# A linear-attention recurrence in blocks: mask on VectorE, scores from 64 rows a head, bonus sums and a compact state on TensorE

## The chip, the core and the metric

The kernel runs on one core of a Trainium2 chip. The metric is the device time of one execution in microseconds (us). A core has TensorE (matrix products into PSUM, with a separate stream of weight loads), VectorE, ScalarE, GpSimd (which can't read PSUM), and SyncE, whose queue (SP) here issues most DMAs.

## The reference

Three stages follow each other: a recurrence with a decaying state (4 batches, 8 heads, 768 steps, head size 48), a mixture of experts with fixed capacity, and a second one with a router over argmax. Only the first matters here:

```python
state = np.zeros((B, H, D, D)); y = np.zeros_like(r)
for t in range(S):
    kt, vt, rt, wt = (k[:, :, t], v[:, :, t], r[:, :, t], w[:, :, t])
    cur = np.einsum('bhd,bhe->bhde', u[None] * kt, vt)
    y[:, :, t] = np.einsum('bhd,bhde->bhe', rt, state + cur)
    state = wt[:, :, :, None] * state + np.einsum('bhd,bhe->bhde', kt, vt)
```

The first expert stage then needs all 3072 rows of y and their gate logits, since its tokens are chosen by a search for a threshold over all rows.

## The kernel before

The recurrence is cut into 24 blocks (`NB`) of 128 steps (`C`), 6 for each batch. Within a block the decay is written as products: `suf` is the suffix product of w (a reversed scan on VectorE), `pf` the prefix product divided by the whole block's product (a second scan), `rp` = r x pf, `kh` = k x suf. Partitions hold 2 heads of 64 (48 used) channels, and 4 such pairs (`NP`) stand side by side, so channel tiles are 128 x 4 x 128. All products on TensorE are fp32.

For block j the steps are, by the functions in `attention`:

- `load`, `load2`: SP fetches channel data (`ch`: w, k, r in two half-height parts, then v for the logits) into one of 3 buffers and token data (`tk`: v, r, k by rows) into one of 4.
- `prep` (L95): the two scans, `rp`, `kh` (GpSimd), the block's product `pe`, and the largest |w| into `WM` for a range check at the end of the kernel.
- `prep2` (L120): ScalarE copies `rp` into a block-diagonal tile `rbd`, so that one 128-row product gives the scores of two heads apart.
- `scores` (L135): 4 products of 256 columns into `pa` (2 banks of PSUM, 2 buffers), 4 transposes of `kh`; ScalarE copies both out (`am`, `kt`). `mask` (L150): GpSimd zeroes `am` above the diagonal.
- `bonus`, `cbv`: r x u x k by rows on GpSimd (`ru`), its sum for each head on VectorE (`cb`), and cb x v on ScalarE, 8 small products (`cv`).
- `vw` (L154): gate logits of v, 3 products, written beside v. `kv` (L171): the state's update: 4 products into `pv`, added to the decayed state on VectorE in two half-height instructions, multiplied by the next block's `pe` on GpSimd (`tmp`, 448 columns, half of them zero).
- `out` (L193): 4 products with the state and 8 with the masked scores into `py` (one buffer), then logits (`le`, `L`) and rows (`y`) on VectorE, and an SP store into DRAM.

The loop over j runs `kv(j)`, `prep(j+2)`, `scores(j+1)`, `mask(j+1)`, `prep2(j+2)`, `vw(j+2)`, `bonus(j+2)`, `out(j)`, `cbv(j+1)`. Each engine works through its instructions in the order in which this code issues them; an instruction that waits holds up those behind it on the same engine. Between the last blocks stand the first steps of the search (`S.mark`, `S.count`, `S.narrow`), and behind the loop the expert stages, whose order is written out by hand with fixed paces.

## Time and profile before

| what | us |
|---|---|
| median of 3 timed runs | 816.48 (812.16 to 817.46) |
| the profiled execution | 810.52 |
| its span, first to last instruction | 808.8 |
| VectorE, busy in the span | 631.8 |
| TensorE, busy in the span | 713.9 |
| GpSimd, busy in the span | 413.1 |
| ScalarE, busy in the span | 352.1 |

The recurrence takes up the first part of the span, to about 233 us, the expert stages the rest. Busy time of an engine includes what an instruction waits after it has started. A share over the whole span says little, since the two parts have different limits; the recurrence is read by itself. Fp32 products appear as two records each, transposes as one.

### The profile page before, as it was taken

The numbers are of one execution on the slowest core, as the hardware profiler recorded it, in microseconds if no ns is written. First come the engines' busy times: TensorE is split into PE (matmuls) and PEld (weight loads), VectorE is DVE, ScalarE is ACT, GpSimd is POOL, SyncE is SP. The second block draws the span as 40 slices with busy tenths as digits, with TensorE's granted clock in tenths as the row PEclk, the third lists the DMA queues.
The fourth block names the chain that finished last, engine by engine and source line by source line (L and its number), as shares of the span: only waits on it lengthen the run. The fifth ranks groups of instructions, "written<-read, shape, count | busy, mean of one in ns | idle before, by whom it ended". The sixth has DMA issues, their size and how long they took to land.

```text
span 808.8 us, 13793 instructions
## 1 busy us (share of the span) xinstructions
PE 713.9 (88%) x4889; PEld 633.7 (78%) x4889; DVE 631.8 (78%) x1575; ACT 352.1 (44%) x756; POOL 413.1 (51%) x371
## 2 busy tenths in 40 slices
PE   6887778878787798999999999999999999999993
PEld 4776667777754577878787878878778999999993
DVE  7999999999978877687876866847776668677770
ACT  3454545545422224333332433323345556666650
POOL 5788876878715413121211212135558766776640
PEclk8898988889899999999999999999999999999998
DMA  8567767667305235251533424264438766776740
GB/s 284 137 177 174 192 163 183 172 173 193 89 31 186 88 99 173 74 183 50 170 104 112 143 74 157 59 206 138 152 126 288 243 224 218 254 255 219 237 161 24
DMA packets 35199, 129.08 MB, mean 160 GB/s; under 512 B 5225, under 2 KB 14580, under 8 KB 35120
## 3 DMA queue, kind: packets, MB, share of 16 engines
q0 software_dynamic: 17568, 83.82, 30.8%
q1 hardware_dynamic: 16832, 43.95, 20.0%
q8 instruction: 40, 0.66, 0.4%
q10 hardware_dynamic: 720, 0.34, 0.2%
q14 instruction: 39, 0.32, 0.1%
HBM read 113.88 MB, written 14.60 MB: 159 GB/s over the span
## 4 chain that ended last, share of the span: by engine, by line
PE 48%; DVE 30%; issue 10%; DMA 5%; POOL 3%; ACT 2%; POOLq 0%; SPq 0%; DVEq 0%; ACTq 0%
PE ph L837 18%; PE po L710 9%; DVE pf L110 5%; PE po L712 4%; PE po L714 4%; PE po L713 4%; DVE suf L104 3%; DMA ch<-in_ch 2%; DVE pe L116 2%; DMA wraw<-in_w1b,wi 2%; DVE pc L107 2%; PE px L1190 2%; DVE rp L112 2%; DVE g L997 2%; PE px L1010 1%
## 5 line engine op out<-in xcount | busy, mean ns | idle before, releaser
L841 ACT ACTIVATE hh<-ph 128x256 fp32r<-128x256 f32 (+3 forms) x160 | 68.4, 428 | 223.4 <-PE ph L837 204.4
L837 PE MATMUL ph<-xh,w1h 128*128 128x256 f32 (+1 forms) x480 | 154.4, 322 | 1.0 <-DVE hl L845 1.0
L837 PE MATMUL ph<-xl,w1h 128*128 128x256 f32 (+1 forms) x480 | 146.2, 305 | 0.5 <-DVE xl L785 0.2
L837 PE MATMUL ph<-xh,w1l 128*128 128x256 f32 (+1 forms) x480 | 146.3, 305 | 0.0
L139 PE MATMUL pa<-rbd,kh 128*128 128x256 f32 x192 | 64.8, 496 | 46.2 <-ACT rbd L125 46.2
L837 PEld LDWEIGHTS ph<-xh,w1h 128*128 128x128 f32 x480 | 90.6, 189 | 10.6 <-issue 5.0
L837 PEld LDWEIGHTS ph<-xl,w1h 128*128 128x128 f32 x480 | 90.8, 189 | 3.1 <-DVE xl L785 1.4
L710 PE MATMUL po<-w2h,hh 128*128 128x384 f32 x272 | 93.1, 489 | 0.0
L837 PEld LDWEIGHTS ph<-xh,w1l 128*128 128x128 f32 x480 | 90.8, 189 | 0.0
L845 DVE SCALAR_TENSOR_TENSOR hl<-ph,hh 128x256 fp32r<-128x256 f32 (+1 forms) x108 | 49.7, 461 | 51.2 <-ACT hh L841 46.7
L139 PEld LDWEIGHTS pa<-rbd,kh 128*128 128x128 f32 x192 | 45.3, 248 | 56.5 <-POOL ru L131 43.0
L713 PE MATMUL po<-w2l,hh 128*128 128x384 f32 x264 | 88.5, 335 | 0.0
L753 ACT CAST w1h<-wraw 128x768 fp32r<-128x768 f32 x88 | 73.2, 833 | 12.5 <-DMA wraw<-in_w1a,ix 8.8
L498 POOL DMA_INDIRECT wraw<-in_w1a,ix x16 | 16.5, 1034 | 121.3 <-issue 53.0
L710 PEld LDWEIGHTS po<-w2h,hh 128*128 128x128 f32 x272 | 49.5, 190 | 28.8
L757 DVE TENSOR_TENSOR w1l<-wraw,w1h 128x768 fp32r<-128x768 f32 x66 | 64.6, 979 | 7.6 <-ACT w1h L753 7.4
L498 POOL DMA_INDIRECT xg<-xd,ix x24 | 31.3, 1305 | 76.2 <-DVE ix L1146 61.1
L757 POOL TENSOR_TENSOR w1l<-wraw,w1h 128x768 fp32r<-128x768 f32 x22 | 41.2, 1876 | 49.5 <-ACT w1h L753 49.4
L169 ACT ACTIVATE cv<-tk,cb 128x56 f32<-128x56 f32 x192 | 47.2, 328 | 39.2 <-DVE cb L166 39.2
L757 DVE TENSOR_TENSOR w2l<-wraw,w2h 128x768 fp32r<-128x768 f32 x44 | 47.8, 1086 | 11.5 <-ACT w2h L753 11.5
L712 PE MATMUL po<-w2h,hh 128*128 128x384 f32 x160 | 55.2, 345 | 0.0
L714 PE MATMUL po<-w2h,hl 128*128 128x384 f32 x160 | 53.8, 337 | 0.1
(350 smaller groups left out, 1766.9 us busy)
## 6 DMA issues: line engine op xcount, KB each, us to landing
tk<-in_tk SPq DMA_DIRECT2D x24, 608.0 KB, 6.6
ch<-in_ch SPq DMA_DIRECT2D x42, 288.9 KB, 5.4
xd<-y SPq DMA_DIRECT2D x24, 193.0 KB, 2.7
x2d<-x SPq DMA_DIRECT2D x8, 579.0 KB, 4.1
ch<-in_ch SPq DMA_DIRECT2D x23, 192.0 KB, 5.8
ch<-in_ch SPq DMA_DIRECT2D x1, 962.5 KB, 8.8
ch<-in_ch SPq DMA_DIRECT2D x1, 770.5 KB, 8.9
ch<-in_ch SPq DMA_DIRECT2D x2, 256.0 KB, 5.1
```

What stands on the lines that cost most here:

```text
L139: nc.tensor.matmul(pa[:, 2 * a:2 * a + 2], t["kh"][:, a], t["rb"][:, a], start=True, stop=True)
L169: nc.scalar.mul(cv[:, h], t["v"][:, DE * h:DE * h + DE], cb[:, h:h + 1])
L498: nc.gpsimd.indirect_dma_start(out=out, out_offset=None, in_=src, in_offset=bass.IndirectOffsetOnAxis(ap=idx, axis=0), bounds_check=bound, ...
L710: mm(o, hh[:, s], w[0][:, hs], start=a, stop=z)
L712: mm(o, hh[:, s], w[0][:, hs], start=a, stop=False)
L713: mm(o, hh[:, s], w[1][:, hs], start=False, stop=False)
L714: mm(o, hl[:, s], w[0][:, hs], start=False, stop=z)
L753: nc.scalar.copy(hi, r)
L757: self.turn[j][q].tensor_tensor(lo, r, hi.bitcast(FT), OP.subtract)
L837: nc.tensor.matmul(ph, a[:, f // 4, k, s], b[:, k], start=(n == 0), stop=(n == 3 * KB - 1))
L841: nc.scalar.activation(hh, ph, AF.Relu)
L845: nc.vector.scalar_tensor_tensor(hl, ph, 0.0, hh.bitcast(FT), op0=OP.max, op1=OP.subtract)
```

## The change

VectorE multiplies the scores in PSUM by a 0/1 mask tile (`msk`) into `am`; the ScalarE copy and the GpSimd selection are gone. Scores are 8 products of 64 rows (one head each) and 128 columns, straight from `kh` and `rp`; `rbd` is gone. The bonus sum is r x k in channel layout (`rk`, GpSimd) times u on TensorE, 4 products of 2 columns, into the logits' bank, copied out with them by ScalarE. The token data loses r and k (1216 to 456 columns). The state is kept for each head in its own half of the partitions: 8 products of 64 weight columns into `pv`, one addition (`s`), one GpSimd product of 224 columns (`tmp`), and two ScalarE copies into a block-diagonal tile `bd` for `out`. The range check is two ScalarE passes with sums (`within`) in place of a reduce on VectorE. `prep` and `prep2` are cut anew, `out` is split into `out`, `logits` and `rows`, and the loop's order changes. The diff, cut:

```diff
...
-            tk = ld.tile([128, TW], FT, name="tk", bufs=4)
...
+            tk = ld.tile([128, VW], FT, name="tk", bufs=4)
             nc.sync.dma_start(tk, d["tk"][j])
-            t["v"], t["rk"] = tk[:, 0:VW], tk[:, VW:].rearrange("p (a c) -> p a c", a=2)
...
-            suf = wk.tile([128, NP, C + 1], FT, name="suf")
+            t["suf"] = suf = wk.tile([128, NP, C + 1], FT, name="suf")
             sufl = suf.rearrange("p a b -> p (a b)")
             nc.vector.tensor_tensor_scan(sufl[:, ::-1], w[:, 1:n + 1][:, ::-1], K["d1r"][:, ::-1], 0.0, OP.mult, OP.add)
             df = d1f[j % 2]
-            pc = wk.tile([128, NP], FT, name="pc")
-            nc.vector.tensor_scalar(pc, suf[:, :, 0], 2.0 ** -100, None, op0=OP.max)
-            nc.vector.reciprocal(df[:, :, 0], pc)
+            nc.vector.tensor_scalar(PE_[:, j], suf[:, :, 0], 2.0 ** -100, None, op0=OP.max)
+            nc.vector.reciprocal(df[:, :, 0], PE_[:, j])
+            t["kh"] = wk.tile([128, NP, C], FT, name="kh", bufs=2)
+            nc.gpsimd.tensor_tensor(t["kh"], k, suf[:, :, 1:], OP.mult)
+
+        def prep2(j):
...
-            nc.vector.tensor_tensor_scan(pf.rearrange("p a b -> p (a b)"), w[:, 0:n], df.rearrange("p a b -> p (a b)"), 0.0, OP.mult, OP.add)
+            nc.vector.tensor_tensor_scan(pf.rearrange("p a b -> p (a b)"), w[:, 0:n], d1f[j % 2].rearrange("p a b -> p (a b)"), 0.0, OP.mult, OP.add)
             t["rp"] = wk.tile([128, NP, C], FT, name="rp", bufs=3)
             nc.vector.tensor_tensor(t["rp"], r, pf[:, :, 0:C], OP.mult)
-            t["kh"] = wk.tile([128, NP, C], FT, name="kh", bufs=2)
-            nc.gpsimd.tensor_tensor(t["kh"], k, suf[:, :, 1:], OP.mult)
-            t["pe"] = wk.tile([128, NP], FT, name="pe", bufs=4)
-            nc.vector.tensor_copy(t["pe"], suf[:, :, 0])
-            nc.vector.tensor_copy(PE_[:, j], suf[:, :, 0])
-            nc.vector.tensor_reduce(WM[:, j:j + 1], w, axis=AX.X, op=OP.max, apply_absolute_value=True)
...
-        def prep2(j):
...
+        def rkm(j):
...
-            rb = rbd[j % 3]
-            t["rb"] = rb
-            nc.scalar.copy(rb[0:64, :, 0], t["rp"][0:64])
-            nc.scalar.copy(rb[64:128, :, 1], t["rp"][64:128])
-
-        def bonus(j):
...
-            rk = t["rk"]
-            ru = wk.tile([128, DM], FT, name="ru")
-            nc.gpsimd.tensor_tensor(ru, rk[:, 0], u, OP.mult)
-            nc.gpsimd.tensor_tensor(ru, ru, rk[:, 1], OP.mult)
-            t["ru"] = ru
+            w, k, r = cuts(j)
+            t["rk"] = wk.tile([128, NP, C], FT, name="rk")
+            nc.gpsimd.tensor_tensor(t["rk"], r, k, OP.mult)
...
+        def within(j):
+
+            w = T[j]["ch"][:, 0:CHW]
+            jk = wk.tile([128, CHW], BF, name="jk", bufs=1)
+            nc.scalar.activation(jk, w, AF.Relu, bias=wmax, accum_out=WM[:, 0, j:j + 1])
+            nc.scalar.activation(jk, w, AF.Relu, scale=-1.0, accum_out=WM[:, 1, j:j + 1])
 
         def scores(j):
             t = T[j]
-            pa = ps.tile([128, 2 * NP, C], FT, name="pa", bufs=2)
+            t["pa"] = pa = ps.tile([128, 2, NP, C], FT, name="pa", bufs=2)
             for a in range(NP):
-                nc.tensor.matmul(pa[:, 2 * a:2 * a + 2], t["kh"][:, a], t["rb"][:, a], start=True, stop=True)
+                for h in range(2):
+                    q = slice(64 * h, 64 * h + 64)
+                    nc.tensor.matmul(pa[:, h, a], t["kh"][q, a], t["rp"][q, a], start=True, stop=True)
...
-            t["am"] = am = wk.tile([128, 2 * NP, C], FT, name="am")
-            nc.scalar.copy(am, pa)
-            if j % NCH < NCH - 1:
...
         def mask(j):
-            am = T[j]["am"]
-            nc.gpsimd.affine_select(am, am, pattern=[[0, 2 * NP], [1, C]], compare_op=OP.is_gt, fill=0.0, base=0, channel_multiplier=-1)
+            t = T[j]
+            t["am"] = am = wk.tile([128, 2, NP, C], FT, name="am")
+            nc.vector.tensor_tensor(am.rearrange("p h a c -> p (h a) c"), t["pa"].rearrange("p h a c -> p (h a) c"),
+                                    msk[:, None, :].to_broadcast([128, 2 * NP, C]), OP.mult)
...
         def vw(j):
...
-            pl = ps.tile([128, H, E], FT, name="pl")
+            pl = ps.tile([128, H, E + 1], FT, name="pl")
             for a in range(3):
-                nc.tensor.matmul(pl, vt[:, a], wg[:, a], start=(a == 0), stop=(a == 2))
-            nc.scalar.copy(t["v"].rearrange("p (h e) -> p h e", e=DE)[:, :, D:], pl)
+                nc.tensor.matmul(pl[:, :, 0:E], vt[:, a], wg[:, a], start=(a == 0), stop=(a == 2))
+            for a in range(NP):
+                nc.tensor.matmul(pl[:, 2 * a:2 * a + 2, E:E + 1], t["rk"][:, a], us[:, a], start=True, stop=True)
+            nc.scalar.copy(t["v"][:, :, D:], pl)
...
         def cbv(j):
             t = T[j]
-            cb = wk.tile([128, H], FT, name="cb")
-            nc.vector.tensor_reduce(cb, t["ru"].rearrange("p (h d) -> p h d", d=D), axis=AX.X, op=OP.add)
             t["cv"] = cv = wk.tile([128, H, DE], FT, name="cv")
             for h in range(H):
-                nc.scalar.mul(cv[:, h], t["v"][:, DE * h:DE * h + DE], cb[:, h:h + 1])
+                nc.scalar.mul(cv[:, h], t["v"][:, h, 0:DE], t["v"][:, h, DE:DG])
...
         def kv(j):
...
+            t = T[j]
+            if j % NCH == NCH - 1:
...
+            t["pv"] = pv = ps.tile([128, H, DE], FT, name="pv")[:, 0:NP]
+            for a in range(NP):
+                for h in range(2):
+                    q = slice(64 * h, 64 * h + 64)
+                    nc.tensor.matmul(pv[q, a], t["kt"][:, a, q], t["v"][:, 2 * a + h, 0:DE], start=True, stop=True)
+
+        def state(j):
...
+            s = wk.tile([128, NP, DE], FT, name="s")
+            if c == 0:
+                nc.vector.tensor_copy(s, t["pv"])
+            else:
+                nc.vector.tensor_tensor(s, t["pv"], t["tmp"], OP.add)
...
+            t1["tmp"] = tmp = wk.tile([128, NP, DE], FT, name="tmp")
+            nc.gpsimd.tensor_tensor(tmp, s, t1["suf"][:, :, 0:1].to_broadcast([128, NP, DE]), OP.mult)
+            t1["bd"] = bd = bds[(j + 1) % 2]
             for h in range(2):
                 q = slice(64 * h, 64 * h + 64)
-                if c == 0:
-                    nc.vector.tensor_copy(s[q, :, h], pv[q, :, h])
-                else:
-                    nc.vector.tensor_tensor(s[q, :, h], pv[q, :, h], t["tmp"][q, :, h], OP.add)
-            tmp = wk.tile([128, NP, 2 * DE], FT, name="tmp")
-            pe = T[j + 1]["pe"]
-            nc.gpsimd.tensor_tensor(tmp, s.rearrange("p a h e -> p a (h e)"), pe[:, :, None].to_broadcast([128, NP, 2 * DE]), OP.mult)
-            T[j + 1]["tmp"] = tmp.rearrange("p a (h e) -> p a h e", h=2)
+                nc.scalar.copy(bd[q, :, h], tmp[q])
 
...
-                    nc.tensor.matmul(py[:, 2 * a:2 * a + 2], t["rp"][:, a], t["tmp"][:, a], start=True, stop=False)
+                    nc.tensor.matmul(py[:, 2 * a:2 * a + 2], t["rp"][:, a], t["bd"][:, a], start=True, stop=False)
                 for h in range(2):
                     o = 2 * a + h
-                    nc.tensor.matmul(py[:, o], t["am"][:, o], t["v"][:, DE * o:DE * o + DE], start=(c == 0), stop=(h == 1 or c == 0))
+                    nc.tensor.matmul(py[:, o], t["am"][:, h, a], t["v"][:, o, 0:DE], start=(c == 0), stop=(h == 1 or c == 0))
...
+        def logits(j):
...
+            nc.vector.tensor_tensor(le, t["py"][:, :, D:], t["cv"][:, :, D:], OP.add)
             nc.vector.tensor_reduce(L[:, j], le.rearrange("p h e -> p e h"), axis=AX.X, op=OP.add)
-            if j == NB - 1:
...
+        def rows(j):
...
-            nc.vector.tensor_tensor(y[:, 0:DM].rearrange("p (h d) -> p h d", d=D), py[:, :, 0:D], t["cv"][:, :, 0:D], OP.add)
...
+        msk = wk.tile([128, C], FT, name="msk", bufs=1)
+        nc.vector.tensor_scalar(msk, K["i32"], 0.0, None, op0=OP.is_gt)
+        us = wk.tile([128, NP, 2], FT, name="us", bufs=1)
+        nc.scalar.dma_start(us, d["us"])
...
+        for t in bds:
...
         prep(0)
         prep2(0)
+        rkm(0)
         load(2)
...
         for j in range(NB):
             if j + 3 < NB:
                 load(j + 3)
                 load2(j + 3)
+            if j + 1 < NB:
+                scores(j + 1)
             kv(j)
             if j == NB - 3:
-                spare = ps.tile([128, 2 * NP, C], FT, name="pa", bufs=2).rearrange("p a b -> p (a b)")
+                spare = ps.tile([128, 2, NP, C], FT, name="pa", bufs=2).rearrange("p h a b -> p (h a b)")
                 s0, s1 = spare[:, 0:512], spare[:, 512:1024]
             if j == NB - 2:
                 g = S.mark(wk, 0, n1, 0)
             if j + 2 < NB:
+                within(j + 2)
                 prep(j + 2)
             if j + 1 < NB:
-                scores(j + 1)
                 mask(j + 1)
             if j == NB - 3:
                 S.span2(wk, s0)
             if j + 2 < NB:
                 prep2(j + 2)
-                vw(j + 2)
-                bonus(j + 2)
+                rkm(j + 2)
             if j == 0:
                 meta_ready()
             out(j)
             if j + 1 < NB:
                 cbv(j + 1)
+            if j + 2 < NB:
+                vw(j + 2)
+            state(j)
+            logits(j)
+            if j == NB - 1:
+                S.count(s1, g, 0, n1)
+                for i in range(S.hot):
+                    nc.tensor.matmul(s0, K["ones"], K["q1"][:, None, :].to_broadcast([128, 4, 128]), start=True, stop=True)
+                S.count(s1, S.mark(wk, n1, NB, 1), n1, NB)
+            rows(j)
...
```

## Rows read from the trace of the kernel before

PE is TensorE, PEld its weight loads, DVE VectorE, ACT ScalarE, POOL GpSimd, SPq SyncE's queue; L104 is line 104 of the kernel before. In the table of stretches the engines come in the order PE, PEld, DVE, ACT, POOL, behind the stretch and its length.

**Rows 1.** Busy us and instructions by engine, granted clock, DMA share, GB/s, by stretch

```profile
0.00:20.00 20.00, 13.25 (x52) 8.91 (x53) 14.82 (x26) 7.43 (x17) 11.75 (x18) 0.83 0.86 284
...
100.00:120.00 20.00, 13.34 (x88) 12.24 (x88) 19.50 (x32) 10.23 (x27) 16.14 (x14) 0.87 0.66 176
...
240.00:260.00 20.00, 13.59 (x114) 7.64 (x114) 17.07 (x56) 4.03 (x7) 10.51 (x9) 1.00 0.50 166
```

**Rows 2.** Chain of waits: start us, length us, engine, tile, line; four suffix scans

```profile
19.98 1.24 DVE suf L104
...
103.84 1.25 DVE suf L104
...
113.21 1.24 DVE suf L104
...
213.66 1.24 DVE suf L104
```

**Rows 3.** Timeline 103 to 111 us, VectorE and GpSimd: start us, length us

```profile
105.77 1.17 POOL L114 TENSOR_TENSOR kh<-ch,suf 128x512 f32<-128x512 f32 x1
...
106.08 1.95 DVE L110 TENSOR_TENSOR_SCAN pf<-ch,d1f 128x516 f32<-128x516 f32 x1
...
106.89 2.02 POOL L152 TENSOR_SCALAR_AFFINE_SELECT am<-am 128x1024 f32<-128x1024 f32 x1
...
108.06 1.39 DVE L112 TENSOR_TENSOR rp<-ch,pf 128x512 f32<-128x512 f32 x1
...
108.88 1.42 POOL L131 TENSOR_TENSOR ru<-tk,u 128x384 f32<-128x384 f32 x1
...
109.38 0.96 DVE L116 COPY pe<-suf 128x4 f32<-128x4 f32 x1
```

**Rows 4.** Timeline near the recurrence's start and end, instructions that nothing holds up

```profile
9.08 0.69 DVE L112 TENSOR_TENSOR rp<-ch,pf 128x512 f32<-128x512 f32 x1 [1.81 <-DMA ch<-in_ch]
9.69 0.16 DVE L116 COPY pe<-suf 128x4 f32<-128x4 f32 x1
...
224.28 0.93 POOL L190 TENSOR_TENSOR tmp<-st,pe 128x448 f32<-128x448 f32 x1 [2.95 <-DVE st L187]
```

**Rows 5.** Groups by line, 40 to 200 us: shapes, count, busy us, mean ns

```profile
L118 DVE TENSOR_REDUCE WM<-ch 128x1 f32<-128x517 f32 x17 | 11.5, 678 | 0.0
...
L212 DVE TENSOR_TENSOR y<-py,cv 128x384 f32<-128x384 f32 x17 | 9.3, 547 | 0.0
...
L187 DVE TENSOR_TENSOR st<-pv,tmp 64x224 f32<-64x224 f32 x22 | 8.4, 383 | 0.1
L205 DVE TENSOR_REDUCE L<-le 128x8 f32<-128x64 f32 x17 | 4.6, 268 | 0.6
L204 DVE TENSOR_TENSOR le<-py,cv 128x64 f32<-128x64 f32 x17 | 3.8, 223 | 0.6
```

**Rows 6.** Timeline of TensorE's products, 119 to 134 us, half clock in the first row

```profile
120.24 3.75 PE L139 MATMUL pa<-rbd,kh 128*128 128x256 f32 x8 [4.11 <-ACT rbd L125]
...
125.40 0.43 PE L199 MATMUL py<-tmp,rp 128*128 128x112 f32 x2
...
128.07 1.10 PE L180 MATMUL pv<-tk,kt 128*128 128x112 f32 x8
129.01 1.91 PE L139 MATMUL pa<-rbd,kh 128*128 128x256 f32 x8
130.75 0.60 PE L143 MATMUL pk<-ident,kh 128*128 128x128 f32 x4
131.19 0.78 PE L160 MATMUL pl<-wg,ch 128*128 128x64 f32 x6
131.81 1.94 PE L202 MATMUL py<-tk,am 128*128 128x56 f32 x16
```

**Rows 7.** DMA issues: the row store's issue; all half-height loads, KB, us to landing

```profile
112.08 0.34 SPq L214 DMA_DIRECT2D xd<-y  x1
...
ch<-in_ch SPq DMA_DIRECT2D x42, 288.9 KB, 5.4
```

More of the change, by code (lines that the diff above doesn't have):

```diff
@@ L39 @@
 DE = D + E
-VW = H * DE
-TW = VW + 2 * DM
+DG = DE + 1
+VW = H * DG
+WMAX = 1.0625
 HOT = 12
@@ L72, in attention @@
         d1f = [wk.tile([128, NP, C + 1], FT, name=f"d1f{i}", bufs=1) for i in range(2)]
-        rbd = [wk.tile([128, NP, 2, C], FT, name=f"rbd{i}", bufs=1) for i in range(3)]
-        stt = [wk.tile([128, NP, 2, DE], FT, name=f"st{i}", bufs=1) for i in range(2)]
+        bds = [wk.tile([128, NP, 2, DE], FT, name=f"bd{i}", bufs=1) for i in range(2)]
         def load(j, *cuts):
@@ L171, in kv @@
         def kv(j):
             t = T[j]
+            if j % NCH == NCH - 1:
+                return
+            t["pv"] = pv = ps.tile([128, H, DE], FT, name="pv")[:, 0:NP]
[4 more added lines that the diff above has]
+        def state(j):
+            t = T[j]
             c = j % NCH
-            if c == 0:
-                t["tmp"] = None
@@ L176, in kv @@
             if c == NCH - 1:
                 return
-            pv = ps.tile([128, NP, 2, DE], FT, name="pv")
-            for a in range(NP):
-                nc.tensor.matmul(pv[:, a], t["kt"][:, a], t["v"][:, 2 * DE * a:2 * DE * a + 2 * DE], start=True, stop=True)
-            s = stt[j % 2]
+            s = wk.tile([128, NP, DE], FT, name="s")
[3 more added lines that the diff above has]
+                nc.vector.tensor_tensor(s, t["pv"], t["tmp"], OP.add)
@@ L195, in out @@
             c = j % NCH
[L196 removed]
+            t["py"] = py = ps.tile([128, H, DE], FT, name="py" if j < NB - 1 else "pv")
             for a in range(NP):
                 if c:
[L199 removed]
+                    nc.tensor.matmul(py[:, 2 * a:2 * a + 2], t["rp"][:, a], t["bd"][:, a], start=True, stop=False)
                 for h in range(2):
                     o = 2 * a + h
[L202 removed]
+                    nc.tensor.matmul(py[:, o], t["am"][:, h, a], t["v"][:, o, 0:DE], start=(c == 0), stop=(h == 1 or c == 0))
+        def logits(j):
+            t = T[j]
             le = wk.tile([128, H, E], FT, name="le")
[L204 removed]
+            nc.vector.tensor_tensor(le, t["py"][:, :, D:], t["cv"][:, :, D:], OP.add)
             nc.vector.tensor_reduce(L[:, j], le.rearrange("p h e -> p e h"), axis=AX.X, op=OP.add)
[L206 to L210 removed]
+        def rows(j):
+            t = T[j]
             y = wk.tile([128, XW], FT, name="y", bufs=3)
[L212 removed]
+            nc.vector.tensor_tensor(y[:, 0:DM].rearrange("p (h d) -> p h d", d=D), t["py"][:, :, 0:D], t["cv"][:, :, 0:D], OP.add)
             nc.gpsimd.tensor_copy(y[:, DM:XW], meta[:, j])
@@ L235, in attention @@
         meta, meta_ready = meta_load()
-        nc.gpsimd.memset(rbd[1], 0.0)
-        for t in stt:
+        for t in bds:
             nc.gpsimd.memset(t, 0.0)
@@ L246, in attention @@
         prep(1)
-        nc.gpsimd.memset(rbd[2], 0.0)
-        bonus(0)
         mask(0)
         prep2(1)
+        rkm(1)
         cbv(0)
         vw(1)
-        bonus(1)
+        within(0)
+        within(1)
         n0, n1 = NB - 3, NB - 2
@@ L313, in host @@
     uc[:, :, :D, 0] = u.reshape(NP, 2, D)
-    return dict(uc=uc.reshape(NP, 128, 1), ch=ch.reshape(NB, 128, CW), tk=tk, u=np.ascontiguousarray(u.reshape(1, DM)),
+    us = np.zeros((2, 64, NP, 2), np.float32)
+    for h in range(2):
+        us[h, :D, :, h] = u.reshape(NP, 2, D)[:, h].T
+    return dict(uc=uc.reshape(NP, 128, 1), us=us.reshape(128, NP, 2), ch=ch.reshape(NB, 128, CW), tk=tk.reshape(NB, C, VW),
                 wg=np.ascontiguousarray(wg.reshape(3, 128, H, E).transpose(1, 0, 2, 3)))
```

45 lines of the change are left out of this document (20 added, 25 removed).

## The prediction

> **What bounds the kernel now.** I read the table of stretches first. In the stretch from 100 to 120 us, which stands for the whole recurrence, VectorE is busy 19.50 of 20 us, TensorE 13.34, GpSimd 16.14 and ScalarE 10.23; the granted TensorE clock averages 0.87 [rows 1]. So the recurrence goes by VectorE. Next the chain of waits, for the period: one suffix scan (line 104) is followed by the next one after 113.21 - 103.84 = 9.37 us. From the scan of block 2 (19.98) to that of block 23 (213.66) there are 21 periods, 193.68 / 21 = 9.22 us on the mean [rows 2]. (The mean is lower because one block in six ends a sequence and has no state update.)
>
> Then the timeline, for what fills those 9.2 us. The reader should lay VectorE's rows beside GpSimd's. The prefix scan `pf` starts at 106.08 and shows 1.95 us; the GpSimd product `kh` runs from 105.77 to 106.94, and the scan ends 1.09 us after that. `rp` shows 1.39 us and ends at 109.45, 0.54 us after the GpSimd selection `am` (106.89 + 2.02 = 108.91). The four-column copy `pe` shows 0.96 us and ends with the GpSimd product `ru` (108.88 + 1.42 = 110.30) [rows 3]. At the start of the kernel, where GpSimd isn't in the way, the same `rp` takes 0.69 and the same `pe` 0.16 us [rows 4]. So a VectorE instruction with two SBUF inputs, or a small copy in SBUF, waits for the GpSimd instruction in progress: some 2.4 us of VectorE's "busy" time per block is such waiting (0.86 on `pf`, 0.70 on `rp`, 0.80 on `pe`). An instruction that reads PSUM doesn't show it: `le` has a mean of 0.223 us over 17 blocks [rows 5].
>
> **The change, part by part.** All figures are for one block; there are 22 periods that can shorten (block 2 to the end of iteration 21).
>
> *VectorE, what goes.* `pe` (0.96), the copy into `PE_` (0.16, by the uncovered `pe`), the range reduce `WM` (0.678), the bonus reduce `cb` (384 columns; by the range reduce's 517 in 0.678, 0.5), one of the two half-height state additions (0.383) [rows 3 to 5]: 2.7 us. *What comes*: the mask product of 1024 columns out of PSUM. No such row exists; `y` (384 columns, PSUM plus SBUF) takes 0.547 and `le` (64) 0.223, or 1.01 ns a column, so 1024 columns make 0.547 + 640 x 0.00101 = 1.20 us. Bounds: the columns alone, 1.04, and 1.40 if two PSUM banks cost a second fixed part of some 0.16; I take 1.20.
>
> *VectorE, what is left.* suf 1.25, two four-column instructions at 0.16, mask 1.20, pf 1.09, rp 0.54 to 0.69, state 0.383, le 0.223, L 0.268, y 0.547: 5.9 us in durations. What GpSimd still does is `kh` (1.17), the new r x k product of the same shape (1.17), and `tmp` with half its columns: 0.93 uncovered at 448 columns [rows 4], so 0.47 to 0.93, I take 0.5; selection and both `ru` are gone. `kh` can only start behind `suf`, then runs beside the mask, which reads PSUM. The r x k product follows it and ends some 2.4 us after `suf`; VectorE reaches `pf` some 1.6 us after `suf` (two small instructions and the mask), so about 0.8 us of waiting stays. 5.9 + 0.8 = 6.7 us. Bounds: 5.9 if nothing waits, and 8.1 if a small instruction waits for all of `kh` (1.0 more) and `suf` for `tmp` (0.4).
>
> *TensorE.* At the full clock, from start to start of the groups: output 128.07 - 125.40 = 2.67, state product 0.94, scores 1.74, transposes 0.44, logits 131.81 - 131.19 = 0.62; sum 6.41 us [rows 6]. Each fp32 product is two records, a transpose one, and an interval is about 0.11 us where the moving side has 128 columns or fewer. After: 16 score records of 128 columns, 1.78 us if they go one by one, 0.9 if the two 64-row halves go side by side. State product: 16 records with 64 weight columns, 1.76 if each costs what a 128-column one does, 0.47 if each costs half and two go at once. Four new products for the bonus sums are 8 records, 0.88. Transposes and output as before. Sum: 5.9 to 8.1. Where the form of the product changes (some four times a block) the overlap of one group with the next may be lost; the state product shows 1.10 us against 0.94 to the next start, so 0 to 0.16 each, 0.64 in all. One block in six has no transposes and state product, and one no state part in the output (2.67 against 1.94 - 0.16), which takes 0.3 to 0.5 off the mean. TensorE's mean then lies between 5.6 and 8.3 us; no row decides, and I take the middle, 7.0.
>
> The Trainium skill, on its page "TensorEngine Tiling (Array Packing)", sections Overview and Key Properties, says that products with at most 64 rows can run up to twice as fast as independent tiles, and also that changing the tiling mode drains the engine. By the first alone the sum would be near 6 us, by the second with nothing gained above 8; no run here shows either yet.
>
> *Clock.* Scores at half clock take 3.75 us instead of 1.91 [rows 6], and those come after waits of some 3 us for `rbd`. These waits go: 7.0 us of work in a period of about that length leaves none. From 240 to 260 us TensorE has only 13.59 busy us of 20 and the granted clock is 1.00 [rows 1], so short gaps don't lower it. I take the full clock.
>
> *ScalarE.* 10.23 of 20 us is 4.8 a block. It loses the copy of the scores (1024 columns) and two `rbd` copies (512 each), and gets two range passes (517 each) and two state copies (224 each): fewer columns, one instruction more. I cost it at nothing; its cover is the 2 us that it idles in a 7 us period. The Trainium skill, "ScalarE: Activation LUTs", section What ACT_TABLE_LOAD costs, gives 280 ns + 0.833 ns a column for an activation with a bias operand, 0.71 us for the first range pass; the sum would be the same, under the cover.
>
> *DMA and queues.* The token load shrinks from 128 x 1216 to 128 x 456 fp32, 608 to 228 KB; the count of DMAs per block stays five, all on SP. SP's load of block j+3 stands behind the row store of block j-1, as before, and takes 5.4 us to land; with three issues of 0.34 us (the store, the load's first two parts) that is 6.4 us, under 7 [rows 7]. At the start the two token loads ahead of block 2's load bring 0.76 MB less, at the 284 GB/s of the first 20 us [rows 1] 2.6 us: the scan at 19.98 should come at about 17.4. The new wait of that load for the range pass on ScalarE lies ahead of a need one period later.
>
> *New waits.* The mask makes VectorE wait for TensorE's scores (before, ScalarE did); behind it stand pf, rp, state, le, L and y. Scores of the next block need only last iteration's rp, and follow the logits, so they are early unless TensorE is the bound. TensorE's bonus products wait for r x k, which is done some 3 us ahead of them. The tail (block 23: marks, mask, output, count) keeps its length: the mask of 1.2 replaces a selection, but the state goes through one more engine.
>
> **Sum.** VectorE 6.7, TensorE 7.0 (5.6 to 8.3), loads 6.4. Two engines so near each other wait for one another at every block; I take 7.1 us a period. 22 x (9.22 - 7.1) = 46.6, plus 2.6 at the start: 810.5 - 49 = 761 for the profiled execution, which shows 810.52 with a span of 808.8. The three timed runs have a median 6 us above that execution and a lowest one 1.6 above; I put 4 on top: **765 us**.
>
> **Rivals.**
> 1. *TensorE becomes the bound, or the waits for GpSimd come back elsewhere.* 64-row records cost full ones and each change of form its 0.16, or a small VectorE instruction waits for `kh`: 8.1 to 8.3 us. For it: no row shows that half-height products cost less. Against: two independent upper ends. 22 x (9.22 - 8.2) = 22; 810.5 - 25 + 4 = 790 us. Chance 0.22.
> 2. *Everything pairs.* TensorE needs 5.6 to 6, `pf` gets ahead of r x k, and the period falls to the 6.4 us of the loads: 810.5 - 62.0 - 2.6 + 4 = 750 us. For it: r x k needs nothing of the scan and could be put anywhere; against: it is queued behind `kh`. Chance 0.12.
> 3. *The other side: the clock.* If the tiled products with few rows don't hold the clock at 2.4 GHz, TensorE's 7.0 us become 14 at 1.2 GHz throughout: 810.5 + 22 x 4.8 = 916 us. It decides from a mean granted clock of 7.0 / 9.22 = 0.76; the stage now has 0.87, with long waits in it that go away. Chance 0.04.
> 4. *The change gives back what it takes* (mask stalls on scores, state copy late, range passes in ScalarE's way), and the period stays over 8.9 us: 808 or more. Nothing on the page asks for it. Chance 0.03.
>
> **How the numbers follow.** 0.59 is left for the forecast, whose own range is 6.6 to 7.7 us a period, 754 to 778. The wide range takes in rivals 1 and 2 up to their given times, 6.3 to 8.2 us a period: 748 to 790; what it leaves out is rivals 3 and 4 and their neighbours. Measurements of this kernel can't tell under 1% (8 us) from no change. Rivals 1 and 2 are faster by more than that; so faster 0.93, same 0.03, slower 0.04.
>
> **What would show it.** In the changed kernel's profile: the period from `suf` to `suf` (7.1); the mask row on VectorE (1.2, and no longer beside `kh`); `pf` near 1.1 plus at most 0.8; the score records' interval (0.11 or half); the granted clock in the recurrence (1.0); the scan of block 2 near 17.4; the stage behind the recurrence as long as before. Wrong would make it: a period over 8 with VectorE waiting on the scores, a clock under 0.9, or a load of `ch` that ends the wait of `suf`.

## The result and the profile after

The changed kernel takes 783.0 us (median, 773.2 to 786.1) against 816.4 us (812.2 to 817.5) for the kernel before in the same runs: a ratio of 0.956, interval 0.948 to 0.964. The forecast was 765 us, its range 748 to 790. The profiled execution is the fastest of the runs, 773.2 us with a span of 771.4; the forecast for the profiled execution, without the 4 us for the medians, was 761.

Four events cut the two spans alike: the suffix scan of block 23, the first narrowed threshold `th` of the first expert stage (line 582 before, 611 after), and the first and last store `x2d`.

| stretch | before, us | after, us | change |
|---|---|---|---|
| start to the scan of block 23 | 213.66 | 167.56 | -46.1 |
| to the narrowed threshold | 19.89 | 22.85 | +3.0 |
| to the first `x2d` store | 89.14 | 91.95 | +2.8 |
| to the last `x2d` store | 245.30 | 245.53 | +0.2 |
| to the end | 240.81 | 243.51 | +2.7 |

So up to that scan the recurrence brought nearly what was forecast (49.2 us, one of the 22 periods of it behind that scan), and 8.7 us of it are given back afterwards. Suffix scans, the changed kernel's timeline of VectorE (they answer to [rows 2]; start, length, engine, line):

```profile
14.70 1.23 DVE L109 TENSOR_TENSOR_SCAN suf<-ch,d1r 128x516 f32<-128x516 f32 x1
...
64.64 1.23 DVE L109 TENSOR_TENSOR_SCAN suf<-ch,d1r 128x516 f32<-128x516 f32 x1 [0.59 <-DMA ch<-in_ch]
71.35 1.23 DVE L109 TENSOR_TENSOR_SCAN suf<-ch,d1r 128x516 f32<-128x516 f32 x1
...
91.98 1.22 DVE L109 TENSOR_TENSOR_SCAN suf<-ch,d1r 128x516 f32<-128x516 f32 x1
98.67 1.23 DVE L109 TENSOR_TENSOR_SCAN suf<-ch,d1r 128x516 f32<-128x516 f32 x1
...
167.56 1.23 DVE L109 TENSOR_TENSOR_SCAN suf<-ch,d1r 128x516 f32<-128x516 f32 x1
```

The step is 6.7 us wherever nothing disturbs it (71.35 - 64.64 = 6.71, 98.67 - 91.98 = 6.69), better than the 7.1 of the forecast. Yet (167.56 - 14.70) / 21 = 7.28 on the mean: the steps from 22.9 to 34.0 and to 43.6 us take 11.07 and 9.63. The table of stretches says why (columns as in [rows 1]):

```profile
20.00:40.00 20.00, 20.00 (x141) 18.65 (x140) 12.17 (x24) 10.05 (x34) 6.21 (x8) 0.57 0.64 146
...
80.00:100.00 20.00, 20.00 (x218) 19.02 (x217) 19.55 (x30) 14.14 (x47) 9.09 (x12) 0.95 0.74 178
...
180.00:200.00 20.00, 16.78 (x128) 11.24 (x129) 10.57 (x45) 0.39 (x2) 0.00 (x0) 0.75 0.06 21
...
240.00:260.00 20.00, 17.94 (x141) 14.25 (x141) 12.82 (x37) 3.66 (x7) 4.46 (x4) 0.91 0.31 106
```

From 80 to 100 us two engines are full at once: TensorE 20.00 and VectorE 19.55 of 20. From 20 to 40 the granted clock is 0.57, TensorE has no idle time, and VectorE falls to 12.17. That is TensorE as the bound, at 1.2 GHz. TensorE's products of one block at 2.4 GHz, from the timeline (answering to [rows 6]):

```profile
85.06 1.16 PE L145 MATMUL pa<-rp,kh 64*128 64x128 f32 x16
86.15 0.66 PE L149 MATMUL pk<-ident,kh 128*128 128x128 f32 x4
86.74 0.68 PE L185 MATMUL pv<-tk,kt 128*64 128x56 f32 x16
87.35 0.47 PE L212 MATMUL py<-bd,rp 128*128 128x112 f32 x2
...
90.07 0.84 PE L165 MATMUL pl<-wg,ch 128*128 128x64 f32 x6
90.75 1.00 PE L167 MATMUL pl<-us,rk 128*128 128x2 f32 x8
91.68 1.05 PE L145 MATMUL pa<-rp,kh 64*128 64x128 f32 x14
```

From start to start: scores 1.09, transposes 0.59, state product 0.61, output 2.72, logits 0.68, bonus 0.93; one block 91.68 - 85.06 = 6.62 us. The same groups at 1.2 GHz, 22 to 34 us:

```profile
22.09 1.19 PE L167 MATMUL pl<-us,rk 128*128 128x2 f32 x8
23.21 2.08 PE L145 MATMUL pa<-rp,kh 64*128 64x128 f32 x16
25.22 1.11 PE L149 MATMUL pk<-ident,kh 128*128 128x128 f32 x4
...
32.47 1.50 PE L165 MATMUL pl<-wg,ch 128*128 128x64 f32 x6
```

Scores 2.01, and from scores to logits 32.47 - 23.21 = 9.26 us instead of 90.07 - 85.06 = 5.01; with logits 1.29 and bonus 1.74 (the next groups start at 33.76 and 35.50), about 12 us a block. VectorE's groups, 40 to 200 us (answering to [rows 5]):

```profile
L122 DVE TENSOR_TENSOR_SCAN pf<-ch,d1f 128x516 f32<-128x516 f32 x19 | 41.3, 2174 | 0.0
L156 DVE TENSOR_TENSOR am<-pa,msk 128x1024 f32<-128x1024 f32 x20 | 23.9, 1196 | 0.0
L109 DVE TENSOR_TENSOR_SCAN suf<-ch,d1r 128x516 f32<-128x516 f32 x19 | 23.3, 1228 | 2.9 <-DMA ch<-in_ch 2.3 <-POOL y L227 0.4
L124 DVE TENSOR_TENSOR rp<-ch,pf 128x512 f32<-128x512 f32 x20 | 13.8, 692 | 0.7
L226 DVE TENSOR_TENSOR y<-py,cv 128x384 f32<-128x384 f32 x21 | 11.5, 548 | 0.0
```

The mask takes 1.196 us (1.20 was estimated), `rp` 0.692 with no wait left in it. Only the prefix scan `pf` still shows more than its own time. Timeline of VectorE and GpSimd (answering to [rows 3]):

```profile
79.95 1.19 DVE L156 TENSOR_TENSOR am<-pa,msk 128x1024 f32<-128x1024 f32 x1
...
80.90 1.28 POOL L130 TENSOR_TENSOR rk<-ch 128x512 f32<-128x512 f32 x1
...
81.06 2.20 DVE L122 TENSOR_TENSOR_SCAN pf<-ch,d1f 128x516 f32<-128x516 f32 x1
```

The scan starts at 81.06, inside `rk`, and ends 1.08 us after `rk` (83.26 against 82.18).

### The profile page after: what moved, and what is told of

The parts are those of the page before. It is cut to its first block, busy times and chain, and to the rows that moved or that the text cites. A ratio compares the mean times of both kernels' runs of the same rounds, so it can differ in the third digit from the quotient of the medians.

```text
span 771.4 us, 14794 instructions
## 1 busy us (share of the span) xinstructions
PE 717.3 (93%) x5433; PEld 639.1 (83%) x5433; DVE 574.6 (74%) x1485; ACT 350.3 (45%) x820; POOL 316.2 (41%) x320
## 4 chain that ended last, share of the span: by engine, by line
PE 50%; DVE 11%; issue 6%; DMA 3%; ACT 2%; POOL 2%; POOLq 0%; ACTq 0%; DVEq 0%
PE ph L866 19%; PE po L739 10%; PE po L741 5%; PE po L743 4%; PE po L742 4%; DMA wraw<-in_w1b,wi 2%; PE px L1219 2%; PE px L1039 2%; DVE g L1026 2%; PE px L807 2%; DVE w1l L786 1%; POOL out L1531 1%; ACT hh L870 1%; DMA xg<-x2d,li 1%; DVE xl L814 1%
## 5 line engine op out<-in xcount | busy, mean ns | idle before, releaser
L739 PE MATMUL po<-w2h,hh 128*128 128x384 f32 x272 | 94.8, 496 | 0.0
L786 DVE TENSOR_TENSOR w1l<-wraw,w1h 128x768 fp32r<-128x768 f32 x66 | 63.0, 955 | 7.8 <-ACT w1h L782 7.3
L741 PE MATMUL po<-w2h,hh 128*128 128x384 f32 x160 | 55.3, 345 | 1.2 <-ACT x L1527 1.2
L215 PE MATMUL py<-tk,am 128*128 128x56 f32 x368 | 52.8, 273 | 0.0
L215 PEld LDWEIGHTS py<-tk,am 128*128 128x128 f32 x368 | 49.9, 200 | 0.2
L742 PEld LDWEIGHTS po<-w2l,hh 128*128 128x128 f32 x264 | 49.9, 189 | 0.2
```

The lines of the kernel that those rows point to most:

```text
L215: nc.tensor.matmul(py[:, o], t["am"][:, h, a], t["v"][:, o, 0:DE], start=(c == 0), stop=(h == 1 or c == 0))
L739: mm(o, hh[:, s], w[0][:, hs], start=a, stop=z)
L741: mm(o, hh[:, s], w[0][:, hs], start=a, stop=False)
L742: mm(o, hh[:, s], w[1][:, hs], start=False, stop=False)
L786: self.turn[j][q].tensor_tensor(lo, r, hi.bitcast(FT), OP.subtract)
```

## Experiments

**Theory.** At 2.4 GHz the period is VectorE's 6.7 us, with TensorE's 6.6 just below it. What is missing is lost while the clock is at 1.2 GHz, and the clock falls around the products that hold few columns or few rows (bonus, 64-row scores). **Rivals:** the clock falls by chance or through idle gaps, whatever runs; or the tail's 3 us come from the new order of the work (a wait), not from the clock; or the prefix scan is simply slow.

**The same kernel again.**

> The changed kernel once more, unaltered, for its spread. If the spells of half clock in the recurrence (22.8 to 39.7 us in its first trace, while TensorE was busy 20.00 of 20 us) are the kernel's own, they lie at the same places again and the suffix scans go from block 2 to block 23 in 152.9 us (14.70 to 167.56) within some 3 us. If they come from outside the kernel, the places and the length move by 5 to 15 us between executions, and with them the time (773 to 786 so far).

781.2 us (778.6 to 790.0), ratio 0.964 (0.957 to 0.971). Its profiled execution has its half-clock spells elsewhere: 0.62 from 60 to 80 us, 0.52 from 180 to 200. The spells move between executions, and from the scan of block 2 to that of block 23 it takes 159.96 us, 7.1 more than the first profile: the second expectation. Over the six timed runs of the changed kernel time goes with the mean granted clock:

| mean granted clock | 0.953 | 0.947 | 0.944 | 0.943 | 0.938 | 0.927 |
|---|---|---|---|---|---|---|
| us | 773.2 | 779.7 | 781.5 | 784.5 | 786.1 | 793.5 |

**Wide bonus products.** Each moves 64 columns, 62 of them zero, into a padded tile (`WB` is 64); nothing else on TensorE changes.

```diff
+        us = wk.tile([128, NP, WB], FT, name="us", bufs=1)
...
-                nc.tensor.matmul(pl[:, 2 * a:2 * a + 2, E:E + 1], t["rk"][:, a], us[:, a], start=True, stop=True)
+                nc.tensor.matmul(pb[:, a], t["rk"][:, a], us[:, a], start=True, stop=True)
```

> The bonus products move 64 columns (62 of them zeros) in place of 2, and one more small ScalarE copy takes the sums out; the result is the same. The records of these products cost 0.12 us each with 2 columns, set by the weight load, so they cost the same with 64. Theory A, the spells of half clock begin behind the bonus products (22.1, 55.8 and 96.7 us in the first trace of the changed kernel) and are brought on by them: the granted clock of the recurrence rises from 0.83-0.97 to 1.0, the early stretch loses no 8 us, time down by 6 to 10 us. Theory B, the spells come from elsewhere (the gaps at the start, a chip that grants what it likes): clock and time stay within 2 us.

773.5 us (769.0 to 783.4), ratio 0.955 (0.948 to 0.963) where the repeat beside it has 0.964: some 8 us less, but the intervals overlap, and the first measurement of the changed kernel had 0.956 too. The times alone don't show a gain; the clock does. Its table of stretches:

```profile
100.00:120.00 20.00, 18.88 (x211) 17.34 (x211) 18.66 (x27) 14.12 (x50) 9.32 (x11) 1.00 0.83 184
120.00:140.00 20.00, 18.60 (x202) 17.50 (x200) 19.38 (x31) 13.40 (x49) 9.30 (x12) 1.00 0.80 174
```

The clock is 1.00 here. Counted in stretches of 0.25 us from 8 us to the scan of block 23, TensorE is at 1.2 GHz for 17 us, against 44 and 52 us in the two profiles of the changed kernel and 65 us in that of the next section, whose recurrence is the same up to there. TensorE isn't busier for it: 18.88 of 20 us, and it has gaps. Timeline:

```profile
97.22 1.16 PE L146 MATMUL pa<-rp,kh 64*128 64x128 f32 x16 [0.71 <-DVE rp L125]
```

The scores wait 0.71 us here and the clock stays at 1.00, so such a gap alone doesn't lower it. One long step is left at the start (13.98 us): the gate weights arrive late, since their transfer is queued behind one that waits for the padding.

**The marks issued late.** `S.mark` of the finished blocks (its `g` takes 1.62 us on VectorE) goes behind the rows of block 22.

```diff
-            if j == NB - 2:
-                g = S.mark(wk, 0, n1, 0)
...
             rows(j)
+            if j == NB - 2:
+                g = S.mark(wk, 0, n1, 0)
```

> The first marks of the search (VectorE, 2.9 us of instructions, ahead of block 23's mask) are issued behind block 22's rows. Theory: the tail grew by 3.0 us because state and mask of the last block wait behind the marks, TensorE stands idle from 178.7 to 180.5 us and runs the last outputs at half clock. Then the tail from the scan of block 23 to the first threshold falls from 22.6 to 17-19 us, and the time by 3 to 6 us. Rival: the marks are needed by the counts right behind the last output, so they only move behind it, and the tail stays within 1 us.

774.4 us (772.9 to 783.4), ratio 0.952 (0.947 to 0.957). What it removes is plain in the changed kernel's timeline of the tail:

```profile
177.38 1.21 DVE L156 TENSOR_TENSOR am<-pa,msk 128x1024 f32<-128x1024 f32 x1
178.51 0.38 DVE L197 TENSOR_TENSOR s<-pv,tmp 128x224 f32<-128x224 f32 x1
```

```profile
178.16 0.56 PE L215 MATMUL py<-tk,am 128*128 128x56 f32 x4
180.46 0.77 PE L212 MATMUL pv<-bd,rp 128*128 128x112 f32 x2 [1.73 <-ACT bd L204]
```

The marks hold VectorE, so mask and state of the last block are late, TensorE idles 1.73 us, and the outputs that follow run at 1.2 GHz (0.77 us a pair instead of 0.47). With the marks late this idle time is gone, but this kernel's profiled execution was its slowest and ran its tail at 1.2 GHz from 185 us on: 23.3 us from the scan to the threshold, no less than with the wait. So by itself it doesn't show what the wait costs.

**Upper and lower rows apart.** The loops of `scores` are swapped, so that products of the upper and the lower 64 rows no longer alternate.

```diff
-            for a in range(NP):
-                for h in range(2):
+            for h in range(2):
+                for a in range(NP):
```

> The eight score products are issued all of the lower half first, then all of the upper half, in place of by turns; nothing else differs. If two 64-row products on different halves run side by side only when they stand next to each other, the 16 records take some 1.75 us in place of 1.09 and the period goes from 6.7 to about 7.3, since TensorE is busy throughout. If 64-row records are simply shorter, both stay as they are.

883.5 us, in its one execution. Its timeline and its table of stretches:

```profile
106.58 3.10 PE L145 MATMUL pa<-rp,kh 64*128 64x128 f32 x16
109.61 1.11 PE L149 MATMUL pk<-ident,kh 128*128 128x128 f32 x4
```

```profile
120.00:140.00 20.00, 20.00 (x118) 18.67 (x119) 9.16 (x14) 8.29 (x27) 5.03 (x7) 0.50 0.48 111
...
200.00:220.00 20.00, 20.00 (x118) 19.22 (x115) 8.37 (x16) 8.65 (x29) 3.79 (x6) 0.50 0.32 72
```

Two things. At the same clock the scores take 3.03 us instead of 2.01, so alternating halves do run side by side. And the clock stays at 0.50 in every stretch of 20 us from 20 to 280 us, with TensorE busy 20.00 of 20 in each: a period of 13.3 us, no idle gap anywhere, and yet it doesn't rise.

**The same with wide bonus products.** Both edits above together.

> The upper rows' scores all behind the lower rows' (which alone left the clock at 0.50 from 20 us to the end of the recurrence, 883 us), with wide bonus products. Theory A, what the products of few columns or rows leave unused decides over the clock: the wide products bring it back for most of the recurrence, the period is 7.0 to 8 us with scores of about 1.5 us, and the time is 785 to 810. Theory B, the clock stays at 0.50 as long as TensorE has no idle time at all: with products of 64 columns that take the same time, nothing changes, 875 to 890.

903.9 us, again one execution, 0.50 throughout again, period 13.4. (Of the 20 us above the kernel with the first edit alone, 13 lie behind the recurrence, where the half clock lasts longer.) Widening one product is no cure in this order, and theory A, as it was written there, is wrong. That a full TensorE always stays at 1.2 GHz (theory B) is wrong too: the changed kernel comes back to 2.4 GHz at 39.8 us from a stretch with no idle time. What sets the rise in one order and prevents it in the other stays open.

**Transposes ahead of the scores.** In `scores` the four transposes are issued first, so that they stand between bonus products and scores; no work is added.

```diff
+            if j % NCH < NCH - 1:
+                pk = ps.tile([128, NP, C], FT, name="pk")
+                for a in range(NP):
+                    nc.tensor.transpose(pk[:, a], t["kh"][:, a], K["ident"])
...
             t["pa"] = pa = ps.tile([128, 2, NP, C], FT, name="pa", bufs=2)
...
-            if j % NCH < NCH - 1:
-                pk = ps.tile([128, NP, C], FT, name="pk")
-                for a in range(NP):
-                    nc.tensor.transpose(pk[:, a], t["kh"][:, a], K["ident"])
...
```

> The four transposes of a block (128 x 128, 0.59 us at full clock) go ahead of its scores, so that they stand between the bonus products and the 64-row scores; the bonus products stay 2 columns wide, and no work is added or left out. In the kernel's traces the falls of the granted clock begin in the bonus products or in the scores right behind them, the rises in the transposes, state and output products. Theory A, the falls need the bonus products and the scores standing next to each other: the mean granted clock of the runs rises from the 0.92 to 0.95 of the changed kernel to 0.96 and more, and the time is 768 to 776. Theory B, the order within a block doesn't matter, only what a block holds in all: clock and time stay where they are, 778 to 786; the scores come 0.6 us later, which can cost VectorE some tenths of a us a block.

768.8 us (765.2 to 784.2), ratio 0.944 (0.938 to 0.950). The granted clock is 0.953 to 0.965 in three of its four runs, and 0.932 in the one that takes 784.2 us; half-clock time in the recurrence of the profiled one is 31 us. Order alone is worth some 12 us between medians from different sets of runs, mostly as theory A had it. In the changed kernel's profile all nine falls of the clock from 9 to 160 us begin in the bonus products or in scores, and eight of the nine rises come in state products or outputs (the other, at 12.5 us, in the logits). But eight of the nine spells are equally long within 0.1 us, so the place of a rise follows from that of the fall and shows no cause by itself.

Nor does every block have a fall. From 50 us on, all ten falls in the two profiles of the changed kernel (six and four) come right behind a block at the border of two sequences, one that lacks the transposes, the state product or the output's part with the state; none comes behind a full block, though its bonus products and scores are the same. In the first profile they stand at 56.9, 97.9 and 138.8 us and at 70.6, 111.5 and 152.5 us, a sequence apart. Before five of the ten TensorE idles for 0.24 to 0.47 us, before the other five no gap shows. That fits theory A's denser products between the thin ones, but no run adds such products to these blocks alone: what lowers the clock there is not shown.

**One bonus product in place of four.** Leaves out the bonus of three head pairs.

```diff
-            for a in range(NP):
-                nc.tensor.matmul(pl[:, 2 * a:2 * a + 2, E:E + 1], t["rk"][:, a], us[:, a], start=True, stop=True)
+            nc.tensor.matmul(pl[:, :, E:E + 1], t["rk"][:, 0], us.rearrange("p a h -> p (a h)"), start=True, stop=True)
```

> Leaves out the bonus of three of the four head pairs: one bonus product of 8 columns in place of four of 2 columns (the output isn't the reference's by that). TensorE loses 3 x 0.24 = 0.73 us a block at full clock (four products take 0.97 us) and 1.3 us at half clock. Theory A, the narrow products let the clock fall (each fall in the changed kernel began within or just behind the four of them): the stretches at half clock go as they did with 64-column products, the period is VectorE's 6.7 us, and the time is 765 to 775. Theory B, the clock falls for another cause and any lighter TensorE helps only by its sum: stretches at half clock remain, with a period of 9.9 us in place of 11.3 us, and the time is 777 to 783.

832.4 us, but the end alone (last `x2d` store to the end) takes 299 us instead of 243, since other rows give other tokens to the experts; neither expectation thought of that. Read to the scan of block 23 only: 168.4 us, as in the changed kernel (167.6), with 55 us at half clock. 0.7 us less of TensorE's work a block brought nothing and didn't hold the clock, which speaks for theory B of that run. Neither the time that the bonus products take nor their mere presence is what costs.

**Mask back on ScalarE and GpSimd.**

```diff
-            nc.vector.tensor_tensor(am.rearrange("p h a c -> p (h a) c"), t["pa"].rearrange("p h a c -> p (h a) c"),
-                                    msk[:, None, :].to_broadcast([128, 2 * NP, C]), OP.mult)
...
+            nc.scalar.copy(am, pa)
+            nc.gpsimd.affine_select(am, am, pattern=[[0, 2 * NP], [1, C]], compare_op=OP.is_gt, fill=0.0, base=0, channel_multiplier=-1)
```

> The mask alone goes back to the way of before: a ScalarE copy of the scores out of PSUM and a GpSimd affine_select in place of the VectorE product (1.20 us a block in the changed kernel's trace). If VectorE sets the full-clock period of 6.7 to 6.9 us (its own sum), it gets shorter only as far as TensorE's 6.6 us: 22 x 0.1 to 0.2 us, 3 to 5 us, time about 778. Rival: GpSimd's select comes behind its products, which alternate with VectorE's scans (prefix scan 2.18 us a block with 1.09 of waiting), the masked scores come late to the outputs, TensorE waits, and the period goes to 7.5 to 8.2 us: 14 to 30 us slower than the changed kernel, 797 to 813. The clock's stretches at half may be other ones, since TensorE would have idle time.

795.1 us (788.4 to 797.5), ratio 0.974 (0.968 to 0.980): the mask is worth some 12 us of the 33. Groups of VectorE, 40 to 180 us:

```profile
L124 DVE TENSOR_TENSOR rp<-ch,pf 128x512 f32<-128x512 f32 x18 | 21.7, 1204 | 0.6
```

`rp` waits again (1.20 us in place of 0.69), and half-clock time grows to 88 us, so some of the 12 us are the clock's. The time lies nearer to the rival's.

**Range check back on VectorE.**

```diff
-            nc.scalar.activation(jk, w, AF.Relu, bias=wmax, accum_out=WM[:, 0, j:j + 1])
-            nc.scalar.activation(jk, w, AF.Relu, scale=-1.0, accum_out=WM[:, 1, j:j + 1])
+            nc.vector.tensor_reduce(WM[:, j:j + 1], w, axis=AX.X, op=OP.max, apply_absolute_value=True)
```

> The range check alone goes back to one VectorE reduction a block (0.7 to 0.75 us by the trace of before) and the two ScalarE passes are gone (ScalarE 14 of 20 us busy with them). If VectorE is full at the full clock (19.55 of 20 us busy), the whole price is on the period: 6.75 + 0.7 = 7.45 us, 22 x 0.7 = 15 us, about 798, less what lies in stretches at half clock, where TensorE's 11 us hide it: 11 to 15 us, 794 to 798. Rival: VectorE's busy time contains 1.09 us of waiting in the prefix scan, and the reduction takes the place of that waiting: under 4 us, 783 to 787.

796.9 us (790.7 to 799.0), ratio 0.977 (0.971 to 0.983). The reduce takes 0.680 us, the undisturbed step is 7.29 instead of 6.71: 0.58 of it is on the period, so VectorE sets the period at 2.4 GHz, as the first expectation had it. Half-clock time is 85 us here, although TensorE has more room: room on TensorE doesn't hold the clock either.

**r times k on VectorE.**

```diff
-            nc.gpsimd.tensor_tensor(t["rk"], r, k, OP.mult)
+            nc.vector.tensor_tensor(t["rk"], r, k, OP.mult)
```

> The product of r and k goes from GpSimd to VectorE, behind the prefix scan and its product. If the prefix scan's 2.18 us is 1.09 us of its own and 1.09 us of waiting while GpSimd works on r times k (1.27 us), VectorE gives 1.09 us back and pays one product of SBUF tiles, 0.69 us: sum 6.35 us, and TensorE's 6.62 us is the bound: period 6.6 us, 22 x 0.1 to 0.2 = 2 to 4 us less, about 780. Rival: the scan takes 2.18 us by itself, then the period rises by 0.69 us to 7.4 us, about 796. The prefix scan's mean decides: 1.1 us or 2.2 us.

Groups of VectorE, 40 to 180 us:

```profile
L122 DVE TENSOR_TENSOR_SCAN pf<-ch,d1f 128x516 f32<-128x516 f32 x19 | 23.2, 1222 | 0.0
...
L130 DVE TENSOR_TENSOR rk<-ch 128x512 f32<-128x512 f32 x18 | 12.3, 684 | 0.0
```

The scan falls from 2.17 to 1.22 us: it was waiting for GpSimd. The shortest repeated step falls to 6.34 us. Yet the time is 784.5 us (774.8 to 788.1), ratio 0.955 (0.949 to 0.961): no gain that can be told. TensorE, whose 6.62 us are now the larger sum, is at 1.2 GHz for 72 us of the recurrence in the profiled execution (788.1 us).

**Wide bonus products, a mended start, late marks.** Gate weights' transfer first, padding zeroed early by GpSimd, 18 warming products instead of 12.

```diff
-HOT = 12
+HOT = 18
...
+        nc.gpsimd.memset(us, 0.0)
...
         nc.scalar.dma_start(wg, d["wg"])
+        nc.scalar.dma_start(us[:, :, 0:2], d["us"])
```

> The wide bonus products again, with the start mended (gate weights' transfer ahead of the bonus weights', the zeros of the wide tile written early by GpSimd, 18 warming products in place of 12) and the marks of the finished blocks issued behind the rows of the next to last block. If the clock is what is left over, the early stretch at half clock (10.9 to 23.9 us with the wide products alone, one step of 13.98 us) goes: 5 to 7 us, and the tail from the last suffix scan to the threshold goes from 21.8 to about 20 us: 773.5 - 5 - 2 = 766, range 763 to 770. Rival: the early fall has nothing to do with the pause between warming products and first scores, and comes again: 770 to 774.

764.9 us (760.7 to 769.9), ratio 0.940 (0.936 to 0.944). The first 40 us run at a clock of 1.00, and the tail, marks late and at 2.4 GHz, takes 16.98 us against 22.85. Timeline of its tail:

```profile
175.20 0.56 PE L219 MATMUL py<-tk,am 128*128 128x56 f32 x4
175.84 0.47 PE L216 MATMUL pv<-bd,rp 128*128 128x112 f32 x2
```

The last output follows the one before it almost at once. So the tail's loss was the wait behind the marks and the clock together. With the marks late the tail took 23.3 us at half clock, so some 6 us are what the clock can cost there; what the wait costs at 2.4 GHz no run shows. Half-clock time up to the scan of block 23 is 20 us.

**The same with r times k on VectorE.** This edit and the one of the section before it together.

> As the kernel above, and r times k on VectorE. With wide bonus products TensorE is 18.75 of 20 us busy at full clock and VectorE 19.1; VectorE's sum goes from 6.75 to 6.35 us a block (prefix scan 1.22 us in place of 2.19, one product of 0.69 us more), TensorE's is about 6.4. Theory: the period is 6.4 to 6.5 us if the clock holds: 18 x 0.3 to 0.4 us, 6 us less than the kernel above, 758 to 762. Rival: a TensorE without idle time loses the clock in stretches, as when this move was made alone: no gain or some us more than the kernel above, 766 to 775.

760.9 us (759.4 to 764.1), ratio 0.935 (0.933 to 0.938), the lowest of all, with 17 us at half clock. The move that alone gave nothing gives 4 us between the medians once the clock holds, with intervals that just meet. The shortest steps are 6.34 us, but the mean from block 2 to block 23 is 146.48 / 21 = 6.98: many of the others end with a wait of `suf` for its load. Groups of VectorE, 40 to 160 us:

```profile
L110 DVE TENSOR_TENSOR_SCAN suf<-ch,d1r 128x516 f32<-128x516 f32 x17 | 20.9, 1227 | 4.5 <-DMA ch<-in_ch 4.1 <-POOL y L231 0.2
```

So the loads are the next limit here.

## Why the prediction was right or wrong

- **VectorE's sum**: the total is right, in part by luck. 6.7 forecast, 6.7 measured in undisturbed steps; mask 1.196 for 1.20; `pf` 2.17 us in all for 1.09 + 0.8, of which 2.17 - 1.22 = 0.95 is the wait. The durations of such a step add up to some 7.07 us; each instruction starts a little before the end of the one ahead, 0.36 us in all, which the forecast, a sum of durations, left out; its shorter `pf` made up for it. That VectorE sets the period is confirmed by the range check put back, the wait by r times k moved.
- **TensorE's sum**: 6.62 for 7.0, inside 5.6 to 8.3. Scores pair (1.09 for 0.9 to 1.78), the state product takes 0.61 (0.47 to 1.76), bonus 0.93 (0.88). A change of form costs little: the whole sum holds four a block. The Trainium skill, "TensorEngine Tiling (Array Packing)", Overview, has up to twice the speed for 64 rows: 1.74 to 1.09 here. Its drain at a change of mode, in Key Properties, can't be seen as a cost of its own in these rows.
- **The period**: 7.1 was taken for two engines close together; undisturbed it is 6.7, on the mean 7.28. A better step and a worse clock nearly cancel, and that is luck too.
- **The start**: 2.6 us gained was forecast; the scan of block 2 stands at 14.70, 5.3 us earlier. The term was sized by the bytes of the token loads alone; where the other 2.7 us come from stays open.
- **The clock**: the step that failed. "I take the full clock" leaned on a stretch of the expert stages with short gaps in it [rows 1], and on waits that go away. The waits did go, and the clock still fell. Before the change TensorE was at half clock for 61 us of the recurrence too, but VectorE was the bound and TensorE had room. How much, the stretch with 13.34 of 20 us overstates: it is the lowest of the recurrence from 20 us on, the others have 14.9 to 17.1. Table of stretches of the kernel before:

```profile
180.00:200.00 20.00, 17.12 (x124) 16.15 (x124) 19.50 (x30) 9.95 (x27) 16.48 (x14) 0.91 0.78 195
```

After the change there are only 44 us of half clock, but on the path. At the undisturbed 6.71 us, 21 steps would end 152.9 - 140.9 = 12 us sooner. The early spell (11.07 and 9.63 us) makes 7.3 of them; not all of the rest is the clock's, since `suf` also waits 2.3 us for loads from 40 to 200 us.
- **The tail "keeps its length"**: wrong by 3.0 us. The marks now stand ahead of the mask on VectorE, and the mask is now ahead of the state: a queue that the text named without counting it. Behind that wait the outputs ran at half clock.
- **The stage behind "unchanged"**: work and code are, but it takes 5.7 us more. From the threshold to the first store TensorE is at half clock for 10.2 us against 3.4 before, in spells that start at 214, 224 and 241 us; they go with 2.8 of it. The 2.7 us at the end have no cause shown: with the same work the repeat has 240.8 us there, as before, and the mended start 244.5.
- **From the profiled execution to the median**: 4 us forecast, 9.8 measured. The profiled execution happened to be the fastest of six; in the repeat the median lies 2.6 us above the profiled one.

In all: 3.1 us less gain to the scan of block 23, 3.0 in the tail, 5.7 behind it and 5.8 more to the median make the 18 us between 765 and 783. (One of the 22 periods lies behind the scan of block 23; counted there, the recurrence misses by 1.0 and the tail by 5.1.) The 783 us lie outside the forecast's own 754 to 778 and inside the wide range only by the room left for rival 1, whose full-cost 64-row records and longer waits didn't come. Rival 3 had the mechanism, half clock on a TensorE without slack, as an event of the whole recurrence; it came in spells, and throughout only in the order with the halves apart (883.5 us; 916 was its price).

## What to carry to other kernels

When a change brings two engines level, the granted clock becomes a term of the sum: give TensorE's time at both levels, and take the time at 1.2 GHz from the stretches before, even where it costs nothing yet. Look at the order of products, not only at their count: in this kernel wider bonus products and transposes moved between thin products cut the time at half clock, and leaving thin products out didn't. A saving on the second engine showed here only together with an edit that held the first one's clock, so try such edits together too. And read a kernel whose clock moves from several profiles: the same recurrence had 44, 52 and 65 us at half clock.

## What the runs showed of the hardware

- TensorE can stay at 1.2 GHz while it is busy without a gap: 20.00 of 20 us and a granted clock of 0.50 in each stretch of 20 us from 20 to 280 us, with the two halves apart. Being busy doesn't bring the clock back by itself, and a gap of 0.71 us with wide bonus products didn't lower it.
- Eight bonus records of 64 columns take hardly longer than eight of 2 (0.99 us from start to start at 2.4 GHz, 88.59 to 89.58 us, against 0.93), and with them less time was spent at half clock: 17, 20 and 17 us in three profiles instead of 44, 52 and 65.
- 64-row products overlap when the halves alternate: 2.01 us against 3.03 for the same 16 records with the halves apart, at the same clock.
- A VectorE scan with two SBUF inputs waits for a GpSimd product in progress: 2.17 us on the mean with it, 1.22 without.
